# Block sums in the order in which they are read, each step with its own place, and the fourth and fifth groups' attention at new places, with whole exponentials

## The chip, the core and the metric

One core of one Trainium2 chip runs the whole kernel. The time is the device time of one execution in microseconds (us); three runs of the kernel before were taken, and one more was profiled. Engines: PE is TensorE (PEld its weight loads), DVE is VectorE, ACT is ScalarE, POOL is GpSimd, and SP issues the transfers. Each engine works through its own list of instructions in order.

## What is computed

```python
# 8 x 8 heads of 576 x 64, cut in chunks of 64 rows
scores = scale * np.matmul(q_c, k_c.transpose(0, 1, 2, 4, 3))
scores = scores - np.max(scores, axis=-1, keepdims=True)
attn = np.exp(scores)
attn = attn / (np.sum(attn, axis=-1, keepdims=True) + 1e-09)
out = np.matmul(attn, v_c)
# its result, 4608 tokens x 512, goes through
h = x @ w_in                # 512 -> 2048
g = h - np.tanh(h)
return g @ w_out            # 2048 -> 512
```

## The kernel before

**Groups, units and slots.** The 4608 tokens are nine groups of 512; `g` counts them from 0, so that the fourth group has `g` = 3 and the fifth `g` = 4. Each group's attention is worked out beside the feed-forward products of the group before it, and the feed-forward products fill PE. From group 2 on they go in *units*: a unit is half a group (256 tokens, `b` = 0 or 1) times a pair of 128-wide pieces of the inner dimension (`j` = 0 to 7), 16 units to a group. Unit `s` is the `s`-th of them, counted from 0 at group 2: group 3's units are 16 to 31, group 4's begin with 32. A unit has a first product (`gemm1`, L701, or `seven`, L716), then on ACT the tanh (L735), on DVE `g = h - tanh(h)` (L742, `shrink`), on POOL three instructions that add and subtract quarters of it (L743 to L745), on ACT and DVE the two float16 halves of the result (L754 and L755, `split`), and some units later the second product (`gemm2`, L774). The first product has two buffers `ph`: the product of unit `s + 2` waits for L742 of unit `s`. The second product goes through blocks that need seven products in place of eight.

**The block sums.** From unit 34 on, the first product goes by seven in place of eight too. It needs sums of blocks of the first weights, eight of them (`j` = 0 to 7), which `Half.seven` makes in seven steps each: two additions on POOL (L549, L551), two more POOL instructions (L554, L555), two more with a cast on ACT (L557, L558, L570), a difference on DVE with a store to memory (L566, L568), another cast (L574), and another difference and store. Seven of the eight are read back later, two units ahead of their use (`load`, L864); the eighth stays. Working room are two `temporary` pairs of pieces and three `stream` pairs, which from unit 34 on take in the sums that are read back.

**The order.** It is written by hand. `at` is a table of slots: slot `32 + 2 s` is worked off behind the first product of unit `s`, slot `33 + 2 s` behind its second product. `ahead` puts the attention steps of groups 2 and 3 at slots, `beside` those of groups 4 to 8. Within an engine nothing overtakes: a cast that stands ahead of a tanh holds the tanh up until what it waits for is there. SP's list holds the transfers in the same order.

**Attention of one half group** has the steps `scores` (PE, L351), `largest` (DVE, L363), `shifted` (DVE, L375), `exponent` (ACT, L379), `totals` (DVE, L385 to L389), `divided` (DVE, L393), `high` (ACT, L399), `transpose` (DVE L404, and two transposing transfers on SP, L408, into `aT`), `split_high` and `split_low` (halves of v), `values` (PE, L351, three products) and `blocks`, `differences`, `rounded` (the result as blocks, on ACT and POOL). For group 4 alone `shifted` and `exponent` are replaced by `by_row`: 16 instructions on ACT, one for each 64 columns, each of which takes its bias from the maximum and gives its sum too (L371, two rows of the trace each).

The line that decides who gets which room:

```python
made_in[j] = half.seven(j, temporary[1 - i % 2] if i else stream[2], stream[i % 2] if j < FC // 2 - 1 else temporary[1], j == FC // 2 - 1)
```

and the steps' places, 6.5 slots apart from sum to sum: `(13 * i - 43) // 2 + k for k in (0, 1, 2, 4, 5, 6, 7)`, where `i` = `j`.

Of the kernel before, what the change touches and what calls it, by code (L numbers as in the profile page):

```python
# [11 lines left out]
F32 = mybir.dt.float32  # L12
# [7 lines left out]
AX = mybir.AxisListType  # L20
# [39 lines left out]
def attn_ffn_kernel(ctx: ExitStack, tc: tile.TileContext, qE, kE, vE, qL, kL, vL, w_in, w_out, out):  # L60
# [211 lines left out]
    class Late:  # L272
# [86 lines left out]
        def largest(self, g, b):  # L359
            d = self.st[g, b]  # L360
            mx = d["mx"] = self.pool.tile([P, 16, 1], F32, name="mx", bufs=2)
            d["s"] = d["ps"].rearrange("p c e hp k -> p (c e hp) k")
            nc.vector.reduce_max(out=mx[:, :, 0], in_=d["s"], axis=AX.X)  # L363
            if g == SEVEN:
                nc.vector.tensor_scalar_mul(mx, mx, -scale)
                d["sm"] = self.pool.tile([P, 16, 1], F32, name="sm", bufs=2)

        def by_row(self, g, b, some):
            d = self.st[g, b]
            for n in some:  # L370
                nc.scalar.activation(d["s"][:, n], d["s"][:, n], AF.Exp, bias=d["mx"][:, n], scale=scale, accum_out=d["sm"][:, n])  # L371

# [53 lines left out]
        def blocks(self, g, b):  # L426
# [248 lines left out]
    class Fast:  # L675
# [251 lines left out]
        def ending(self):  # L927
# [39 lines left out]
            store(nc.scalar, 0, left)  # L967

    def in_seven(g, b, j):
        return (g, b, j // 2) != (SEVEN, 0, 0) and (g, b, j // 6) != (NG - 1, 1, 1)  # L970

    def beside(att, at, g):

        o = 2 * FC * (g - FAST)

        def put(unit, part, f, *args):
            at[o + 2 * unit + part].append(lambda: f(*args))

        put(-4, 0, att.halves, g, 0)
        late = g == SEVEN  # L980
        put(4 - 2 * late, late, att.halves, g, 1)
        put(10, 0, lambda: powers.update({g: half.power_of(g)}))
        for b, u in enumerate((3, 11)):
            first = g == SEVEN and not b
            put(u + 1 + first, 1, att.scores, g, b)
            put(u + 2 + first, 0, att.largest, g, b)
            if g == SEVEN:
                slots = range(2 * first + 1, 6)
                for i, k in enumerate(slots):
                    some = range(16 * i // len(slots), 16 * (i + 1) // len(slots))  # L990
                    put(u + 2 + k // 2, k % 2, att.by_row, g, b, some)
            else:
                put(u + 3, 0, att.shifted, g, b)
                put(u + 3, 1, att.exponent, g, b)
            put(u + 4 + (g == SEVEN), 0, att.totals, g, b)
            put(u + 5, 0, att.divided, g, b)
            put(u + 5, 1, att.high, g, b)
            put(u + 6, 0, att.transpose, g, b)
            put(u + 6, not first, att.split_high, g, b)
            put(u + 7 - first, first, att.split_low, g, b)  # L1000
            put(u + 8, 0, att.values, g, b)
            put(u + 8, 1, att.blocks, g, b)
            put(u + 9, 0, att.differences, g, b, 0)
            put(u + 9, 1, att.differences, g, b, 1)
            put(u + 10, 1, att.rounded_high, g, b, 1)
            put(u + 10, 1, att.rounded_low, g, b, 1)
            put(u + 11, 1, att.rounded_high, g, b, 0)
            put(u + 11, 1, att.rounded_low, g, b, 0)
            if g + 1 < NG:
                for i in range(2):  # L1010
                    p = FIRST[g + 1] + 2 * b + i, 2 * b + i
                    put(u + 2 + i, 1, att.load, *p, "q")
                    put(u + 4 + i, 1, att.load, *p, "k")
                    put(u + 7, 1, att.load, *p, "v")
        put(6 - late, late, att.spread, g)
        put(6 - late, 1, att.greatest, g)

    def ahead(att, at, g):
# [9 lines left out]
        late, before = g == FAST, g == SEVEN - 1
        if not late:
            put(-3, 0, att.halves, g, 0)  # L1030
            put(3, 1, att.halves, g, 1)
        put(4 if late else 6, -0.5 if late else 0, att.spread, g)
        put(4 if late else 6, -0.5 if late else 1, att.greatest, g)
        put(14 if late else 9, 1, lambda: powers.update({g: half.power_of(g)}))
        put(6, 0, lambda: xs.update({g: new_half_x()}))
        for b, u in enumerate((3, 13) if late else (6, 14)):
            spaced = late and not b
            other = u + 3 if spaced else u + 2 if late else u + 1
# [3 lines left out]
            u += late - before * (1 + b)  # L1042
            put(u + 2, before and b, att.scores, g, b)
            for i in (2 * b, 2 * b + 1):
# [6 lines left out]
            else:  # L1051
# [306 lines left out]
```

## Time and profile before

| | us |
|---|---|
| median of three runs | 790.15 (788.72 to 790.75) |
| the profiled execution, its time | 790.28 |
| the profiled execution, its span | 788.0 |
| PE busy | 769.9 |
| POOL busy | 531.7 |
| DVE busy | 627.8 |
| ACT busy | 497.8 |

The span runs from the first instruction to the last; 2.3 us of the execution lie around it. In rows of the trace a line such as L742 is a line of the kernel before; `x24` counts merged instructions; what stands in brackets is idle time ahead of the instruction and what ended it. PEclk 1.00 is TensorE's clock at 2.4 GHz, and a stretch of 0.93 had some of its time at 1.2 GHz. A matmul's duration is from its start to its modelled end, so two that follow each other overlap in the rows; the time that one costs is the distance of two starts.

### The profile page before, as it was taken

Reading aid. Unit: us, or ns where it says so; the run is one execution under the profiler, and the core shown is the slowest. Engines: PE = TensorE matmul, PEld = TensorE weight load, DVE = VectorE, ACT = ScalarE, POOL = GpSimd, SP = SyncE. Lnnn points to the kernel's source line nnn. Section 1 sums busy time; section 2 is a strip of 40 time slices with the busy share of each in tenths; the row PEclk is TensorE's granted clock in tenths of the full one; section 3 lists DMA queues with packets and bytes.
Section 4 is the critical chain, followed back from the end, with each engine's and each line's share of the span. In section 5 each row is a group of like instructions: output and inputs, shape, how many; then the busy total and the mean of one; then the engine's idle time right before and its main releaser. Section 6 shows DMA issues by size and latency. Waiting matters only on the chain.

```text
span 788.0 us, 23812 instructions
## 1 busy us (share of the span) xinstructions
PE 769.9 (98%) x10037; PEld 666.5 (85%) x10037; DVE 627.8 (80%) x1034; ACT 497.8 (63%) x862; POOL 531.7 (67%) x598
## 2 busy tenths in 40 slices
PE   8999999999999999979899999999999999999997
PEld 4878885666788888868799999999999999999996
DVE  5896998888698898667578797979797979796665
ACT  6887988556465454573856666666666666666553
POOL 1100002586678888869786979797979796979763
PEclk9999999999999999999999999999999999999999
DMA  9854441210232233234254545455545452435120
GB/s 349 320 188 161 161 161 53 82 27 2 81 81 96 81 115 89 67 66 136 82 166 148 161 135 163 134 162 128 167 130 155 151 176 65 154 61 155 55 83 28
DMA packets 78059, 98.02 MB, mean 124 GB/s; under 512 B 34944, under 2 KB 42112, under 8 KB 77952
## 3 DMA queue, kind: packets, MB, share of 16 engines
q1 hardware_dynamic: 77520, 95.84, 39.3%
q8 instruction: 79, 1.29, 0.7%
q10 hardware_dynamic: 432, 0.66, 0.2%
q14 instruction: 28, 0.23, 0.1%
HBM read 76.02 MB, written 13.11 MB: 113 GB/s over the span
## 4 chain that ended last, share of the span: by engine, by line
PE 48%; POOL 4%; DVE 2%; issue 1%; ACT 1%; DMA 0%; POOLq 0%; DVEq 0%; ACTq 0%
PE ph L716 23%; PE po L774 22%; PE psa L351 2%; PE po L938 1%; POOL xl L743 1%; PE ph L701 1%; POOL wl L443 1%; POOL xh L452 0%; DMA aT<-a 0%; POOL xl L745 0%; POOL wh L558 0%; POOL xh L437 0%; ACT wl L754 0%; DVE xl L742 0%; POOL xl L744 0%
## 5 line engine op out<-in xcount | busy, mean ns | idle before, releaser
L743 POOL TENSOR_TENSOR xl<-xl 128x256 f32<-128x256 f32 x111 | 153.3, 1381 | 93.5 <-DVE xl L742 93.2
L735 ACT ACTIVATE t<-ph,sig 128x512 f32<-128x512 f32 x112 | 77.0, 687 | 138.5 <-DVE ph L731 113.9
L716 PE MATMUL ph<-xh,wl 128*128 128x128 f16 x1608 | 115.3, 220 | 2.5 <-DVE xl L742 2.5
L716 PE MATMUL ph<-xh,wh 128*128 128x128 f16 x1530 | 110.9, 220 | 0.3 <-DVE ph L726 0.3
L742 DVE SCALAR_TENSOR_TENSOR xl<-ph,sig,t 128x512 f32<-128x512 f32 x112 | 83.2, 742 | 25.3 <-ACT t L735 25.1
L716 PEld LDWEIGHTS <-wl 128*128 128x128 f16 x1608 | 96.4, 98 | 3.3 <-issue 2.7
L716 PEld LDWEIGHTS <-wh 128*128 128x128 f16 x1530 | 95.2, 98 | 3.1 <-DVE ph L726 1.4
L774 PEld LDWEIGHTS <-gh 128*128 128x128 f16 x924 | 88.0, 98 | 11.1 <-issue 1.5
L701 PE MATMUL ph<-xh,wh 128*128 128x256 f16 x804 | 94.4, 275 | 0.9 <-DVE xl L742 0.9
L774 PEld LDWEIGHTS <-wl 128*128 128x128 f16 x882 | 85.5, 98 | 9.7
L755 DVE SCALAR_TENSOR_TENSOR gl<-xl,to_g,gh 128x896 f16<-128x896 f32 x68 | 83.5, 1228 | 8.4 <-ACT gh L754 8.4
L774 PE MATMUL po<-wl,gh 128*128 128x256 f16 x610 | 88.1, 273 | 0.9 <-DVE wl L787 0.9
L701 PEld LDWEIGHTS <-wh 128*128 128x128 f16 x804 | 78.8, 99 | 11.3 <-issue 1.6
L745 POOL TENSOR_TENSOR xl<-xl 128x256 f32<-128x256 f32 x111 | 83.4, 752 | 0.0
L754 ACT ACTIVATE gh<-xl,to_g 128x896 f16<-128x896 f32 x68 | 70.9, 1043 | 19.7 <-POOL xl L745 19.4
L774 PE MATMUL po<-wl,wl 128*128 128x256 f16 x549 | 82.1, 273 | 0.0
L725 DVE TENSOR_TENSOR ph<-ph,t 128x128 f32<-128x128 f32 x76 | 22.7, 299 | 59.0 <-ACT t L721 58.6
L774 PE MATMUL po<-wh,wl 128*128 128x256 f16 x333 | 60.0, 274 | 0.0
L755 DVE SCALAR_TENSOR_TENSOR wl<-xl,to_g,wl 128x896 f16<-128x896 f32 x44 | 54.7, 1244 | 6.3 <-ACT wl L754 6.3
L615 PE MATMUL ph<-xh,wh 128*128 128x512 f16 (+2 forms) x252 | 59.3, 377 | 0.4 <-ACT xh L269 0.4
L744 POOL TENSOR_TENSOR xl<-xl 128x128 f32<-128x128 f32 x111 | 59.2, 533 | 0.0
L754 ACT ACTIVATE wl<-xl,to_g 128x896 f16<-128x896 f32 x44 | 45.9, 1042 | 19.1 <-POOL xl L745 18.0
(235 smaller groups left out, 1680.2 us busy)
## 6 DMA issues: line engine op xcount, KB each, us to landing
wl<-kept SPq DMA_DIRECT2D x118, 256.0 KB, 3.6
raw<-w_in SPq DMA_DIRECT2D x16, 512.0 KB, 3.7
raw<-w_out SPq DMA_DIRECT2D x16, 512.0 KB, 5.1
xl<-qL SPq DMA_DIRECT2D x28, 256.0 KB, 3.8
rawv<-vL SPq DMA_DIRECT2D x28, 256.0 KB, 2.9
rawk<-kL SPq DMA_DIRECT2D x28, 256.0 KB, 4.6
out<-wl SPq DMA_DIRECT2D x55, 128.0 KB, 1.9
kept<-wl SPq DMA_DIRECT2D x14, 256.0 KB, 2.3
```

What stands on the lines that cost most here:

```text
L615: nc.tensor.matmul(ph, lhsT=w[:, kc * P:(kc + 1) * P], rhs=x[b][:, kc, cols], start=(k == 0), stop=(k == 3 * KC - 1))
L701: nc.tensor.matmul(self.ph[:, 1 - f::2, :], lhsT=half_w[fc][:, w, kc * P:(kc + 1) * P], rhs=rhs, start=(k == 0), stop=(k == 3 * KC - 1))
L716: nc.tensor.matmul(ph[:, o], lhsT=a[:, w, i * P:(i + 1) * P], rhs=x[v][:, m, i * P:(i + 1) * P], start=(n == "P5" and k == i == 0), stop=( ...
L725: nc.vector.tensor_add(ph[:, 3], ph[:, 3], c[:, 2])
L735: nc.scalar.activation(t, self.ph, AF.Tanh, scale=self.powers[0])
L742: nc.vector.scalar_tensor_tensor(out=u[:, :4], in0=self.ph, scalar=sig, in1=t, op0=ALU.mult, op1=ALU.subtract)
L743: engine.tensor_add(u[:, 4:6], u[:, 1:3], u[:, 0:4:3])
L744: engine.tensor_add(u[:, 6], u[:, 1], u[:, 2])
L745: engine.tensor_sub(u[:, 0:4:3], u[:, 0:2], u[:, 2:4])
L754: nc.scalar.activation(gh, u, AF.Copy, scale=powers[1])
L755: nc.vector.scalar_tensor_tensor(out=gl, in0=u, scalar=powers[1], in1=gh, op0=ALU.mult, op1=ALU.subtract)
L774: nc.tensor.matmul(place[m], lhsT=part[:, self.SUM[m]], rhs=w[m][:, o], start=first, stop=(last and part is gl), skip_group_check=True)
```

## The change

The sums are made in the order 2, 3, 4, 5, 6, 7, 0, 1, in which the fifth group's first half reads them, each step at a slot of its own and with its own two rooms (`SUMS`; counted from slot 64). The attention steps of groups 3 and 4 get tables of slots (`FOURTH`, counted from slot 32, and `FIFTH`, from 64). Groups 5 to 8 (`LATER`) and group 2 keep their slots. `by_row` goes: group 4 has `shifted`, one `exponent` and `totals` with its own sum like the others. The room of group 4's first result is `stream[1]` in place of `stream[2]`.

```diff
             nc.vector.reduce_max(out=mx[:, :, 0], in_=d["s"], axis=AX.X)
-            if g == SEVEN:
-                nc.vector.tensor_scalar_mul(mx, mx, -scale)
-                d["sm"] = self.pool.tile([P, 16, 1], F32, name="sm", bufs=2)
-
-        def by_row(self, g, b, some):
-            d = self.st[g, b]
-            for n in some:
-                nc.scalar.activation(d["s"][:, n], d["s"][:, n], AF.Exp, bias=d["mx"][:, n], scale=scale, accum_out=d["sm"][:, n])
...
-            if g != SEVEN:
-                d["sm"] = self.pool.tile([P, 16, 1], F32, name="sm", bufs=2)
-                nc.vector.reduce_sum(out=d["sm"][:, :, 0], in_=d["s"], axis=AX.X)
-            sm = d["sm"]
+            sm = d["sm"] = self.pool.tile([P, 16, 1], F32, name="sm", bufs=2)
+            nc.vector.reduce_sum(out=sm[:, :, 0], in_=d["s"], axis=AX.X)
...
-            d["f"] = [place_of(*n, F32) for n in (stream[2] if (g, b) == (SEVEN, 0) else temporary[0])]
+            d["f"] = [place_of(*n, F32) for n in (stream[ROOM] if (g, b) == (SEVEN, 0) else temporary[0])]
...
+    FOURTH = {'halves': [-6, 7], 'spread': [12], 'greatest': [13], 'power': [17], 'room': [10], 'split': [19, 31], 'scores': [14, 29], 'load_qk': [14, 32], 'largest': [15, 29], 'shifted': [15, 29], 'exponent': [18, 30], 'totals': [18, 32], 'divided': [20, 32], 'high': [22, 34], 'transpose': [23, 35], 'values': [27, 41]}
+    SUMS = {2: (2, 0, [-21, -21, -19, -17, -10, -9, -7]), 3: (3, 1, [-14, -14, -13, -12, -8, -8, -7]),
...
+    ROOM = 1
...
-    def make_in(i, j):
+    def make_in(j):
         if j not in made_in:
-            made_in[j] = half.seven(j, temporary[1 - i % 2] if i else stream[2], stream[i % 2] if j < FC // 2 - 1 else temporary[1], j == FC // 2 - 1)
+            temp, place = SUMS[j][:2]
+            made_in[j] = half.seven(j, *((stream + temporary)[i] for i in (temp, place)), j == FC // 2 - 1)
         next(made_in[j])
...
-    steps = [[(13 * i - 43) // 2 + k for k in (0, 1, 2, 4, 5, 6, 7)] for i in range(FC // 2)]
...
+    for j, (_, _, steps) in SUMS.items():
+        for k in steps:
+            at[o + k].append(lambda j=j: make_in(j))
```

Three places on the engines, as the two programs order them. Behind line 380 the lines of the kernel after stand 10 lower: its tanh is L725, its splits L744 and L745, its `shrink` L732, the casts of a sum L560 and L564, `high` L389.

ACT from unit 23's tanh (L735) to unit 25's, before. `psa` are the scores, a cast L570 or L574 belongs to a sum, L399 is `high`, L330 and L331 come behind unit 25's split:

```order
L735 ACTIVATE t<-ph,sig 128x512
L754 ACTIVATE wl_2496<-xl,to_g 128x896
L371 ACTIVATE psa,sm<-psa,mx 128x64 x11
L570 CAST wl_4521<-wh_4383 128x512
L735 ACTIVATE t<-ph,sig 128x512
L754 ACTIVATE wl_2498<-xl,to_g 128x896
L399 CAST a<-psa 128x2x8x64
L574 CAST wl_4520<-wh_4382 128x512
L735 ACTIVATE t<-ph,sig 128x512
L754 ACTIVATE gh<-xl,to_g 128x896
L330 ACTIVATE rawv<-rawv,to 128x1024
L331 CAST wl_1707<-rawv 128x1024
```

and now, from the whole exponential (L371) at the end of unit 22 on; the first cast is that of sum 7, the second of sum 0:

```order
L371 ACTIVATE psa<-psa 128x1024
L725 ACTIVATE t<-ph,sig 128x512
L744 ACTIVATE wl_2496<-xl,to_g 128x896
L564 CAST wh_4426<-wl_4134 128x512
L725 ACTIVATE t<-ph,sig 128x512
L744 ACTIVATE wl_2498<-xl,to_g 128x896
L560 CAST wl_4559<-wh_4454 128x512
L330 ACTIVATE rawv<-rawv,to 128x1024
L331 CAST wl_1707<-rawv 128x1024
L725 ACTIVATE t<-ph,sig 128x512
L744 ACTIVATE gh<-xl,to_g 128x896
L389 CAST a<-psa 128x2x8x64
```

The 11 rows of the exponential between unit 23's split and unit 24's tanh are gone; `split_high` (L330, L331) stands ahead of unit 25's tanh, `high` (L389) behind it.

DVE in units 31 and 32, before: L566 is a sum's difference, L387 to L389 finish the totals, L393 divides, L404 makes the low half that is transposed, the second L742 is unit 32's:

```order
L742 SCALAR_TENSOR_TENSOR xl<-ph,sig,t 128x512
L755 SCALAR_TENSOR_TENSOR wl_2497<-xl,to_g,wl_2496 128x896
L566 TENSOR_TENSOR wh_5113<-wh_4924,wh_5113 128x512
L387 TENSOR_SCALAR sm<-sm 128x16
L388 RECIPROCAL sm<-sm 128x16
L389 TENSOR_SCALAR sm<-sm 128x16
L393 TENSOR_TENSOR psa<-psa,sm 128x1024
L755 SCALAR_TENSOR_TENSOR wl_2499<-xl,to_g,wl_2498 128x896
L404 TENSOR_TENSOR a<-psa,a 128x2x8x64
L742 SCALAR_TENSOR_TENSOR xl<-ph,sig,t 128x512
```

and now:

```order
L732 SCALAR_TENSOR_TENSOR xl<-ph,sig,t 128x512
L745 SCALAR_TENSOR_TENSOR wl_2497<-xl,to_g,wl_2496 128x896
L376 TENSOR_REDUCE sm<-psa 128x16
L377 TENSOR_SCALAR sm<-sm 128x16
L378 RECIPROCAL sm<-sm 128x16
L379 TENSOR_SCALAR sm<-sm 128x16
L383 TENSOR_TENSOR psa<-psa,sm 128x1024
L745 SCALAR_TENSOR_TENSOR wl_2499<-xl,to_g,wl_2498 128x896
L732 SCALAR_TENSOR_TENSOR xl<-ph,sig,t 128x512
L394 TENSOR_TENSOR a<-psa,a 128x2x8x64
```

The sum's difference is gone from here, the totals have their own sum over the row (L376), and unit 32's `shrink` (now L732) stands ahead of the low half (now L394).

ACT in unit 18, where the second half of group 2 is finished (L789 to L794), before:

```order
L735 ACTIVATE t<-ph,sig 128x512
L754 ACTIVATE gh<-xl,to_g 128x896
L574 CAST wl_3957<-wh_3825 128x512
L789 ACTIVATE wl_3249<-po_3484,undo_g 128x512
L790 ACTIVATE wh_3250<-po_3485,undo_g 128x256
L794 ACTIVATE wl_2493<-po_3486,undo_g 128x256
L735 ACTIVATE t<-ph,sig 128x512
```

and now:

```order
L744 ACTIVATE gh<-xl,to_g 128x896
L779 ACTIVATE wl_3246<-po_3480,undo_g 128x512
L780 ACTIVATE wh_3247<-po_3481,undo_g 128x256
L784 ACTIVATE wl_2493<-po_3482,undo_g 128x256
L564 CAST wl_3829<-wl_3692 128x512
L560 CAST wl_4066<-wh_3901 128x512
L725 ACTIVATE t<-ph,sig 128x512
```

The cast of a sum (L574) stood ahead of the three readings of `po`, and now two such casts stand behind them.

## Rows read from the trace of the kernel before

**Rows 1.** PE's waits by releaser, 228 to 400 us (total, times, longest)

```profile
PE psa L351 <- DVE wl L340: 2.6, 1, 2.6
PE ph L716 <- DVE xl L742: 2.5, 1, 2.5
PE psa L351 <- issue: 1.4, 1, 1.4
PE psa L351 <- DMA aT<-a: 1.1, 2, 0.9
PE po L774 <- DVE wl L787: 0.9, 2, 0.7
PE ph L701 <- DVE xl L742: 0.9, 1, 0.9
```

**Rows 2.** Windows: busy us of PE, PEld, DVE, ACT, POOL, PEclk, DMA share, GB/s

```profile
375.00:400.00 25.00, 22.46 (x229) 20.25 (x230) 15.76 (x23) 18.33 (x48) 20.02 (x24) 0.93 0.36 101
400.00:750.00 350.00, 350.00 (x5864) 329.70 (x5864) 281.71 (x512) 220.12 (x326) 288.64 (x320) 1.00 0.46 136
```

**Rows 3.** PE's timeline, 290 to 405 us: start, us, instruction, [idle before]

```profile
321.79 2.78 PE L701 MATMUL ph<-xh,wh 128*128 128x256 f16 x24
...
326.70 2.78 PE L701 MATMUL ph<-xh,wh 128*128 128x256 f16 x24
...
354.76 0.64 PE L351 MATMUL psa<-aT,wl 64*64 64x64 f16 x32 [0.86 <-DMA aT<-a]
355.34 4.10 PE L701 MATMUL ph<-xh,wh 128*128 128x256 f16 x24
...
392.32 0.80 PE L716 MATMUL ph<-xh,wl 128*128 128x128 f16 x6 [2.54 <-DVE xl L742]
...
397.50 0.50 PE L716 MATMUL ph<-xh,wh 128*128 128x128 f16 x6
397.84 1.17 PE L716 MATMUL ph<-xh,wl 128*128 128x128 f16 x18
```

**Rows 4.** ACT's timeline, 335 to 405 us

```profile
338.81 0.69 ACT L735 ACTIVATE t<-ph,sig 128x512 f32<-128x512 f32 x1
```

**Rows 5.** DVE's timeline, 335 to 405 us

```profile
349.00 1.21 DVE L404 TENSOR_TENSOR a<-psa,a 128x1024 f16<-128x1024 f32 x1
```

**Rows 6.** ACT's groups by form, 240 to 400 us: busy, mean ns | idle before

```profile
L754 ACT ACTIVATE wl<-xl,to_g 128x896 f16<-128x896 f32 x15 | 15.6, 1041 | 15.1 <-POOL xl L745 15.1
...
L371 ACT ACTIVATE psa<-psa,mx 128x64 f32<-128x64 f32 x32 | 9.2, 286 | 4.6 <-DVE mx L365 3.8
...
L574 ACT CAST wl<-wh 128x512 f16<-128x512 f32 x6 | 3.7, 619 | 8.7 <-POOL wh L558 8.7
...
L330 ACT ACTIVATE rawv<-rawv,to 128x1024 f32<-128x1024 f32 x2 | 2.3, 1143 | 0.0
...
L379 ACT ACTIVATE psa<-psa 128x1024 f32<-128x1024 f32 x2 | 2.0, 1010 | 0.4 <-DVE psa L375 0.4
```

**Rows 7.** DVE's groups by form, 240 to 400 us

```profile
L742 DVE SCALAR_TENSOR_TENSOR xl<-ph,sig,t 128x512 f32<-128x512 f32 x27 | 20.1, 744 | 19.8 <-ACT t L735 19.7
...
L755 DVE SCALAR_TENSOR_TENSOR gl<-xl,to_g,gh 128x896 f16<-128x896 f32 x12 | 15.1, 1258 | 3.0 <-ACT gh L754 3.0
L566 DVE TENSOR_TENSOR wl<-wh,wl 128x512 f16<-128x512 f32 x12 | 14.6, 1214 | 0.0
...
L375 DVE TENSOR_TENSOR psa<-psa,mx 128x1024 f32<-128x1024 f32 x2 | 2.5, 1232 | 0.1
```

**Rows 8.** POOL on tile xl, 240 to 400 us: min/median/max ns, first and last start

```profile
L743 POOL TENSOR_TENSOR xl<-xl x28: 714/1170/1582, 240.6 to 396.9; 128x256 f32<-128x256 f32 x28
L744 POOL TENSOR_TENSOR xl<-xl x28: 443/453/1313, 241.3 to 398.5; 128x128 f32<-128x128 f32 x28
L745 POOL TENSOR_TENSOR xl<-xl x28: 719/723/1711, 241.7 to 398.9; 128x256 f32<-128x256 f32 x28
```

**Rows 9.** POOL's groups by form, 240 to 400 us

```profile
L549 POOL TENSOR_TENSOR wh<-wh 128x512 f32<-128x512 f16 x7 | 8.1, 1150 | 0.0
```

More of the change, by code (lines that the diff above doesn't have):

```diff
@@ L972, in beside @@
     def beside(att, at, g):
[L974 to L1008, printed above, removed]
@@ new lines, in beside, with put @@
+        o, keys = 2 * FC * (g - FAST), FIFTH if g == SEVEN else LATER
+        def put(name, f, *args, half=0, nth=0):
+            k = keys[name][half]
+            k = k[nth] if isinstance(k, tuple) else k
+            at[o + k].append(lambda: f(*args))
+        for b in range(2):
+            put("halves", att.halves, g, b, half=b)
+        put("power", lambda: powers.update({g: half.power_of(g)}))
+        for b in range(2):
+            for name in ("scores", "largest", "shifted", "exponent", "totals", "divided", "high", "transpose", "split_high", "split_low", "values", "blocks"):
+                put(name, getattr(att, name), g, b, half=b)
+            for i in range(2):
+                put("differences", att.differences, g, b, i, half=b, nth=i)
+            for i in range(2):
+                for part in "high", "low":
+                    put("rounded", getattr(att, "rounded_" + part), g, b, 1 - i, half=b, nth=i)
@@ L1011, in beside @@
                     p = FIRST[g + 1] + 2 * b + i, 2 * b + i
[L1012 to L1016, printed above, removed]
+                    for n in "qkv":
+                        put("load_" + n, att.load, *p, n, half=b, nth=i)
+        put("spread", att.spread, g)
+        put("greatest", att.greatest, g)
     def ahead(att, at, g):
@@ L1026, in put, with place @@
             at[o + 2 * unit + part].append(lambda: f(*args))
[L1028 to L1034, printed above, removed]
+        if g == SEVEN - 1:
+            def place(name, f, *args, half=0):
+                at[o + FOURTH[name][half]].append(lambda: f(*args))
+            for b in range(2):
+                place("halves", att.halves, g, b, half=b)
+            place("spread", att.spread, g)
+            place("greatest", att.greatest, g)
+            place("power", lambda: powers.update({g: half.power_of(g)}))
+            place("room", lambda: xs.update({g: new_half_x()}))
+            for b in range(2):
+                place("split", att.split, g, b, half=b)
+                for i in (2 * b, 2 * b + 1):
+                    place("split", att.load, FIRST[g + 1] + i, i, "v", half=b)
+                place("scores", att.scores, g, b, half=b)
+                for i in (2 * b, 2 * b + 1):
+                    place("load_qk", att.load, FIRST[g + 1] + i, i, "qk", half=b)
+                for name in ("largest", "shifted", "exponent", "totals", "divided", "high", "transpose"):
+                    place(name, getattr(att, name), g, b, half=b)
+                at[o + FOURTH["values"][b]].insert(0, lambda b=b: (att.values(g, b), att.result(g, b)))
+            return
+        put(4, -0.5, att.spread, g)
+        put(4, -0.5, att.greatest, g)
+        put(14, 1, lambda: powers.update({g: half.power_of(g)}))
         put(6, 0, lambda: xs.update({g: new_half_x()}))
-        for b, u in enumerate((3, 13) if late else (6, 14)):
-            spaced = late and not b
-            other = u + 3 if spaced else u + 2 if late else u + 1
+        for b, u in enumerate((3, 13)):
+            spaced = not b
+            other = u + 3 if spaced else u + 2
             put(other, -0.5 if spaced else 1, att.split, g, b)
@@ L1041, in ahead @@
                 put(other, 1, att.load, FIRST[g + 1] + i, i, "v")
-            u += late - before * (1 + b)
-            put(u + 2, before and b, att.scores, g, b)
+            u += 1
+            put(u + 2, 0, att.scores, g, b)
             for i in (2 * b, 2 * b + 1):
```

13 lines of the change are left out of this document (6 added, 7 removed).

## The prediction

> **What bounds the kernel now.** I read the windows first, then PE's waits, then the timelines around them. From 400 to 750 us PE is busy 350.00 of 350 us at full clock, with DVE busy 282 and POOL 289 [rows 2]: nothing can be won there unless products are left out, and the change leaves none out. What can be won lies before 400 us, where PE waits eight times, 9.4 us in all [rows 1], and where its clock fell twice.
>
> The waits say who was late. In the first half of group 4, unit 24's tanh begins at 338.81 [rows 4]. That unit's first product started 4.91 after unit 23's at 326.70 and took 2.62 (24 products, 0.109 apart: 4.91 is 45 of them), so it was done at 334.2: the tanh was 4.6 late, with 11 rows of the exponential ahead of it on ACT. Behind it everything on ACT and DVE slid: a `ph` was still in use (0.9, L742), then the low half of v was missing (2.6, L340), then the transposed low half of the scores (0.9 of the 1.1, aT) [rows 1, 3]. In the second half the same 16 rows end as 2.5 us before unit 34's product (L742), and 1.4 + 0.9 fall around 307 to 320 us, in unit 18's finish and behind it.
>
> The clock: the 24 products at 355.34 take 4.10 where the same took 2.78 at 321.79 [rows 3], 1.3 more, right behind the long wait; and from 392.32 to 397.50 there are 24 small products (0.0557 apart: 6 take 0.34 from 397.50 to 397.84) and 21 of 0.109, 3.6 at full clock, which took 5.2: 1.6 more, right behind the 2.5 us wait. The window there shows 0.93 [rows 2]: some of it at 1.2 GHz.
>
> A third piece hides in how rows are drawn: a matmul's end is modelled 0.16 behind the next one's possible start (24 × 0.109 = 2.62 against 2.78), so each of eight waits costs 0.16 more than its bracket, 1.3. **All that can go: 9.4 + 2.9 + 1.3 = 13.6 us.** The profiled execution took 790.28, 0.13 above the median, so the floor is 776.7 there and 776.6 by the median.
>
> **What the change does to these, part by part.**
>
> *The exponential in one.* 32 rows L371 of 0.286 and as many readings of the sum go from ACT; two L379 of 1.01 come [rows 6]. DVE gets, twice, one L375 of 1.23 [rows 7] and one row sum of the same 1024 columns, taken alike, less one small multiplication: about 2 us each time. DVE hides it as long as L742 is in time: it sat idle 19.8 us ahead of 27 of them [rows 7], and a `shrink` may end 7.2 - 1.4 = 5.8 us after its product's end plus tanh and itself before the product after the next one wants its `ph` (2.29 + 2.62 + 2.29 between them).
>
> *First half of group 4, counted from unit 22's first product (0).* Without waits unit 27's first product ends at 5 × 4.91 + 2.62 = 27.2, and the three `values` products follow at once: that is the deadline. Durations are the groups' means, tanh 0.69 and split 1.04 on ACT, L742 0.74 and L755 1.26 on DVE [rows 4, 6, 7], about 0.1 less where instructions follow closely. DVE: unit 22's L742 ends at 4.1, the split of 21 at 5.5, maximum and shift at 7.9, two differences of sums at 10.1, L742 of 23 at 10.8. ACT: exponential to 9.0, tanh 23 to 9.6 (due 7.5, allowed to be 5.8 late). DVE goes on: split 11.9, totals 14.2, a difference 15.3, L742 of 24 at 16.0, split 17.1, division 18.3. POOL: 23's three instructions and the next sum's three end at 16.1, whereupon ACT casts it (16.6), splits v (18.7), does tanh 25 (19.3), split 20.3 and `high` 21.3; DVE's low half of the scores ends at 22.6 and that of v at 24.3. In the trace the last wait for aT ended at 354.76, 4.6 after L404 ended at 350.2 [rows 3, 5]; so aT is whole at 27.2, just at the deadline. The `ph` wait and the v wait are gone with 3 to 4 us to spare; the wait for aT is 0 give or take 1.5. I take 0.5 of it as left. It must not bring the clock down: behind the 0.9 us wait before unit 27's product [rows 1] no stretch ran slow.
>
> *Unit 18.* ACT's cast L574 sat 8.7 us idle in six of them for POOL's L558 [rows 6]; one stood ahead of the readings of `po`. Two casts now stand behind them and need sums that POOL finished a unit before. The readings come about 2 us earlier, and with them L742, POOL and group 3's last result: 0.9 and 1.4 go. The price, two casts of 0.62 ahead of tanh 19, lies within the 5.8.
>
> *Second half of group 4.* Unit 34's product is due 12 × 4.91 + 2.0 (scores and `values`) = 60.9 after 0. Its `ph` needs L742 of unit 32, which now stands ahead of the low half, with no rows and no difference before it. POOL sets it: the four `differences` and the two `rounded_low` (about 3.5 and 4) push unit 31's three instructions to 55.6; split on ACT, tanh 32, L742: 58.6. 2.3 to spare, so 2.5 us and the slow clock behind it go.
>
> *Sums and POOL.* The same 48 instructions, but seven units (20 to 26) now carry 18 of them: 18 × about 1.0 (L549 takes 1.15, the smaller ones less [rows 9]), 7 × 2.35 for the three of L743 to L745 at their medians [rows 8], and 2.4 for a finish make 37 against 34.4. POOL falls 3 us behind; its result is asked for a unit later (the split, then a second product three units on), so PE does not see it.
>
> *Group 3.* PE lost 0.2 there. The transposes move from slot 52 to 55 with `values` still at 59: 9.8 us for 4.6 and what DVE is late. 0.
>
> *SP.* Loads of q and k move ahead of those of v, and the read-back of the third sum now waits for POOL's rounding (room `stream[1]`) ahead of the second half's transposes. By the reckoning above POOL rounds at 53, `high` is ready at 58: nothing waits. If POOL were 5 us later, the transposes would slip the same 5 minus 2.7 of slack at `values`.
>
> **Sum.** 790.28 - 13.6 + 0.5 = 777.2, by the median 777.0.
>
> **Rivals.**
>
> *The gap at the first `values` stays.* For it: aT meets its deadline with nothing to spare on a chain of some 25 instructions, and DVE has 12 us of work in the 12 us from 4 to 16. Then 2 to 3.7 us of waiting come back, and the slow clock behind them, 1.3: 3.3 to 5.0 on the floor of 776.7, **780.0 to 781.7**; with the `ph` wait too (0.9 and its 0.2), 782.8.
>
> *It moves and does not go.* For it: every step stands in another row, and lateness before went from ACT to DVE to PE. Both large gaps stay with their clock, and only unit 18's 2.3 + 0.3 go: **787.7**, within 0.3% (2.4 us), which is about what a measurement of this kernel can tell from no change. Against it: the cause, ACT's rows, is not there any more.
>
> *Slower: POOL sets the pace.* Its three instructions take 2.35 at the medians, but 4.6 at their longest [rows 8]. Sums, blocks and roundings now stand shoulder to shoulder from unit 20 to 31. Were all twelve units at the longest, POOL would lose 12 × 2.25 = 27; some 8 of it are hidden by the lag, and 19 against 13.1 gained make **796**. It decides from a mean of about 4.1 a unit on. Against it: half of the L744 and L745 are at 0.45 and 0.72. The rows show L743 between 0.71 and 1.58. The Trainium skill ("SBUF — State Buffer", section "SBUF: two separate sides") has a reason: DVE with two inputs in SBUF and POOL reading SBUF lock each other out for a whole instruction. By that rule the added shift and row sum, which read PSUM, would cost POOL nothing, while the 0 to 3 differences L566 more in these units would block it for up to 3 × 1.2, which alone gives 777 to 778. No row here has the two alone.
>
> **Chances.** Forecast 0.66 (775.0 to 779.5: below, the floor of 776.6 less the 1.4 by which the lowest of three runs lay under the median, rounded down; above, a wait of some 2.5 us without the slow clock); the gap stays 0.18; moves 0.08; POOL sets the pace 0.05; 0.03 for others, half of them faster than the floor by something not seen. The range 775.0 to 784.0 takes in the forecast and the first rival (782.8, and 1.2 for the spread of runs upward), 0.84. Faster by over 0.3%: 0.66 + 0.18 + 0.03 = 0.87; the same 0.08; slower 0.05.
>
> **What would show it.** Right: PE without a wait over 0.5 us from 260 to 750 us, no window under clock 1.00 there, unit 34's product starting near 378 in place of 392, tanh 24 within 1 us of its product's end, the last read of `po` in unit 18 followed by casts. Wrong: a wait of `values` for aT or v over 1.5 us (first rival), L742 or `ph` waits in units 27 to 34 (second), or POOL busy without a pause from 315 to 385 us with a mean of the three instructions over 4 us (third).

## The result, and the profile after

| | median of runs, us | lowest to highest | runs |
|---|---|---|---|
| before | 790.45 | 788.72 to 791.30 | 4 |
| changed | 778.45 | 778.03 to 779.02 | 4 |

The ratio is 0.985, with a 95% interval of 0.983 to 0.987: 12.0 us faster, where 13.1 was forecast (777.0, range 775 to 784). The profiled execution took 779.02 with a span of 776.1, 11.9 shorter than the span before. The same shows on PE alone, without what lies at the two ends of the span: from unit 0's first product to the last matmul of the program it took 555.2 us before (227.92 to 783.09) and 543.1 after (227.74 to 770.87), 12.0 less.

In the changed kernel every line after 379 stands 10 lower: the tanh is L725, shrink's DVE line L732, its POOL lines L733 to L735, the split L744 and L745, the products L691 and L706. Of PE's waits before 400 us, eight with 9.4 us [rows 1], and one of 0.3 near the end, these are left (220 to 760 us; total, times, longest):

```profile
PE psa L351 <- DMA aT<-a: 1.2, 2, 0.7
PE po L764 <- DVE wl L777: 0.3, 1, 0.3
PE ph L706 <- DVE ph L716: 0.3, 1, 0.3
```

The last one is that of 0.3, as before. The windows that answer to [rows 2], with PE busy, then PEld, DVE, ACT and POOL, and the granted clock:

```profile
375.00:400.00 25.00, 25.00 (x445) 23.18 (x443) 19.82 (x33) 15.14 (x23) 20.03 (x23) 1.00 0.57 166
400.00:750.00 350.00, 349.68 (x5727) 329.20 (x5725) 283.75 (x516) 219.28 (x323) 285.98 (x318) 1.00 0.46 135
```

No window up to 750 us is under 1.00 any more. PE's timeline of the changed kernel, at the places that answer to [rows 3] (start, us, instruction, [idle before]):

```profile
275.86 0.71 PE L351 MATMUL psa<-aT,wl 64*64 64x64 f16 x64 [0.71 <-DMA aT<-a]
277.09 0.45 PE L351 MATMUL psa<-aT,wl 64*64 64x64 f16 x32 [0.52 <-DMA aT<-a]
...
320.48 2.79 PE L691 MATMUL ph<-xh,wh 128*128 128x256 f16 x24
...
345.06 2.78 PE L691 MATMUL ph<-xh,wh 128*128 128x256 f16 x24
347.77 0.98 PE L351 MATMUL psa<-aT,wl 64*64 64x64 f16 x96
...
381.65 0.50 PE L706 MATMUL ph<-xh,wl 128*128 128x128 f16 x6
```

All 96 products of group 4's first `values` now run in one piece, 27.3 behind unit 22's first product, and unit 34's product begins 61.2 behind it. What is new is at 275.86: group 3's first `values` wait for aT, 0.71 and 0.52. That is the place which the prediction priced at nothing.

### The profile page after: what moved, and what is told of

It reads as the page before. It is cut to its first block, busy times and chain, and to the rows that moved or that the text cites. A ratio compares the mean times of both kernels' runs of the same rounds, so it can differ in the third digit from the quotient of the medians.

```text
span 776.1 us, 23750 instructions
## 1 busy us (share of the span) xinstructions
PE 764.6 (99%) x10034; PEld 663.8 (86%) x10037; DVE 633.1 (82%) x1036; ACT 486.9 (63%) x800; POOL 532.5 (69%) x598
## 4 chain that ended last, share of the span: by engine, by line
PE 89%; DVE 5%; DMA 2%; ACT 2%; POOL 1%; issue 1%; SPq 0%; POOLq 0%; ACTq 0%; DVEq 0%
PE po L764 30%; PE ph L706 23%; PE ph L691 11%; PE po L636 10%; PE ph L605 9%; PE psa L351 4%; PE psa L186 1%; PE po L928 1%; DMA raw<-w_out 1%; DMA q<-qE 1%; DMA aT<-a 0%; DVE wl L745 0%; PE psa L247 0%; DVE w L144 0%; ACT s L221 0%
## 5 line engine op out<-in xcount | busy, mean ns | idle before, releaser
L733 POOL TENSOR_TENSOR xl<-xl 128x256 f32<-128x256 f32 x111 | 150.4, 1355 | 80.1 <-DVE xl L732 79.9
L725 ACT ACTIVATE t<-ph,sig 128x512 f32<-128x512 f32 x112 | 77.0, 687 | 145.6 <-DVE ph L721 114.8
L706 PE MATMUL ph<-xh,wl 128*128 128x128 f16 x1608 | 114.7, 219 | 0.0
L706 PE MATMUL ph<-xh,wh 128*128 128x128 f16 x1530 | 110.3, 219 | 0.3 <-DVE ph L716 0.3
L706 PEld LDWEIGHTS <-wh 128*128 128x128 f16 x1530 | 94.6, 98 | 3.1 <-DVE ph L716 1.4
L764 PEld LDWEIGHTS <-gh 128*128 128x128 f16 x924 | 88.0, 98 | 10.2 <-issue 0.5
L706 PEld LDWEIGHTS <-wl 128*128 128x128 f16 x1608 | 95.9, 98 | 0.6
L691 PE MATMUL ph<-xh,wh 128*128 128x256 f16 x804 | 93.1, 273 | 0.0
L745 DVE SCALAR_TENSOR_TENSOR gl<-xl,to_g,gh 128x896 f16<-128x896 f32 x68 | 84.3, 1239 | 9.9 <-ACT gh L744 9.9
L732 DVE SCALAR_TENSOR_TENSOR xl<-ph,sig,t 128x512 f32<-128x512 f32 x112 | 83.1, 742 | 10.0 <-ACT t L725 9.8
L691 PEld LDWEIGHTS <-wh 128*128 128x128 f16 x804 | 78.1, 98 | 9.7 <-issue 0.5
L744 ACT ACTIVATE gh<-xl,to_g 128x896 f16<-128x896 f32 x68 | 70.9, 1042 | 24.1 <-POOL xl L735 22.5
L735 POOL TENSOR_TENSOR xl<-xl 128x256 f32<-128x256 f32 x111 | 81.7, 736 | 0.0
L745 DVE SCALAR_TENSOR_TENSOR wl<-xl,to_g,wl 128x896 f16<-128x896 f32 x44 | 57.6, 1309 | 6.8 <-ACT wl L744 6.8
L744 ACT ACTIVATE wl<-xl,to_g 128x896 f16<-128x896 f32 x44 | 45.9, 1042 | 20.7 <-POOL xl L735 17.0
```

What stands on the lines that cost most here:

```text
L691: nc.tensor.matmul(self.ph[:, 1 - f::2, :], lhsT=half_w[fc][:, w, kc * P:(kc + 1) * P], rhs=rhs, start=(k == 0), stop=(k == 3 * KC - 1))
L706: nc.tensor.matmul(ph[:, o], lhsT=a[:, w, i * P:(i + 1) * P], rhs=x[v][:, m, i * P:(i + 1) * P], start=(n == "P5" and k == i == 0), stop=( ...
L725: nc.scalar.activation(t, self.ph, AF.Tanh, scale=self.powers[0])
L732: nc.vector.scalar_tensor_tensor(out=u[:, :4], in0=self.ph, scalar=sig, in1=t, op0=ALU.mult, op1=ALU.subtract)
L733: engine.tensor_add(u[:, 4:6], u[:, 1:3], u[:, 0:4:3])
L735: engine.tensor_sub(u[:, 0:4:3], u[:, 0:2], u[:, 2:4])
```

## The experiments

The change has three parts that can be had apart: the exponentials in one (E), the sums' order, steps and places with their room (S), and the new slots of groups 3 and 4 (T; in the code FOURTH and FIFTH). Order, steps and places of the sums were not taken apart from each other. All eight combinations exist; medians, and in brackets what E is worth at that place:

| | slots before | slots new |
|---|---|---|
| sums before, by row | 790.25 (kernel before) | 787.50 |
| sums before, E | 788.52 (-1.7) | 782.89 (-4.6) |
| sums new, by row | 784.50 | 782.57 |
| sums new, E | 780.11 (-4.4) | 778.45 (-4.1) |

Alone the three give 1.7, 5.8 and 2.8, 10.2 in sum; all at once give 12. E is worth 1.7 alone, and 4.1 to 4.6 wherever one of the others stands beside it. The kernel before stood at 790.25, 789.32, 790.57 and 788.95 in the four sets of runs that follow, so that 1 us between sets means nothing.

A part of these medians is PE's clock and not the order. Each execution has its mean granted clock on record: 0.992 to 0.998 in every one of the kernel before for which it is listed, 0.999 or 1.000 in those of the change, and both in three of the combinations. The sums alone took 782.67 at 1.000 and 784.30 to 785.54 below it, the slots alone 785.33 at 1.000 and 787.29 to 788.51 below it, the change with the old sums 782.17 and 782.23 at 1.000, 783.54 and 784.71 below it. At full clock throughout, E is worth 2.6 beside the new sums (782.67 to 780.11) and 3.1 beside the new slots (785.33 to 782.20), the first number of each pair from one execution, and 4.1 beside both. So E is worth more beside the others than alone, but by less than the table says, and the sum of 10.2 depends on how often the clock fell.

The `diff` blocks of this section give each edit in short, not the lines of the programs.

**Without the exponentials in one.** Where `by_row` is put back, `totals` loses its row sum again for this group.

```diff
-  "shifted", "exponent"                 (group 4)
+  by_row: 16 rows in three pieces at slots 13, 14, 14; in five at 28 to 31
```

> The changed kernel, with the fourth group of the fast part (the program's SEVEN) again taking its exponentials by row: 16 rows of 0.29 us on ACT for each half, at the slots of the one exponential (first half) and at slots 28 to 31 (second); DVE loses the shift and the row sum. Theory A (ACT's rows are what made PE wait): the first half has 4.6 us on ACT where 1.0 stands, 3.6 late against a deadline met with nothing to spare, less the 2.4 us that DVE no longer does ahead of totals: 1 to 3.5 us of waits at the first values or the ph behind them come back, with 1.3 of half clock where one is over 2.5, so 780 to 784. Theory B (the places in the tables are what counts): PE sees nothing, 778 to 779.

Measured 782.57 (782.31 to 782.88; ratio to before 0.991, 0.989 to 0.994), 4.1 more than the change. PE's timeline of this run, where `by_row` moves the numbers back (L774 the second product, L716 the small ones):

```profile
352.39 0.60 PE L774 MATMUL po<-wl,gh 128*128 128x256 f16 x4 [0.31 <-DVE wl L787]
353.69 0.81 PE L774 MATMUL po<-wl,gh 128*128 128x256 f16 x6 [0.70 <-DVE wl L787]
...
385.67 0.50 PE L716 MATMUL ph<-xh,wl 128*128 128x128 f16 x6 [2.35 <-DVE xl L742]
```

3.4 of waits and three restarts of 0.16 are 3.8 of the 4.1. So the size is theory A's, the place is not: the first `values` of group 4 don't wait at all here, 1.0 falls close behind them (L787), and it is unit 34's `ph` that is late. New slots and new sums together cover these `values` even with 16 rows on ACT; either one without the other doesn't (1.6 and 1.3, and 1.4, in two runs below).

**Only the exponentials in one**, in the kernel before.

```diff
-  by_row at slots 13 to 15 and 27 to 31
+  shifted at 13 and 27, exponent at 14 and 28, and the row sum in totals
```

> The kernel before, with nothing changed but the exponentials of that group: one shift on DVE, one exponential on ACT and one row sum on DVE, at the slots where the first rows stood. Theory A: the waits of 2.6, 0.9, 0.9 and most of the 2.5 us go with their half clock, 6 to 9 us in all; unit 18's waits (0.7 and 1.4) stay: 781 to 784. Theory B: 788 to 790.

Measured 788.52 (788.15 to 790.27, 10 runs; ratio 0.9986, 0.9976 to 0.9997, or 1.1 us): theory B's number. The rows by themselves are not the cause on which I had laid the lateness. The waits (PE's, 228 to 400 us; numbers 5 lower than before):

```profile
PE ph L711 <- DVE xl L737: 2.9, 1, 2.9
PE psa L351 <- issue: 1.4, 1, 1.4
PE psa L351 <- DMA aT<-a: 1.2, 1, 1.2
PE psa L351 <- DVE wl L340: 1.2, 1, 1.2
PE po L769 <- DVE wl L782: 0.9, 2, 0.7
PE psa L351 <- DVE xh L419: 0.3, 1, 0.3
```

Unit 34's wait has even grown, from 2.5 to 2.9, and the first `values` still wait 2.4. What took the rows' place there, ACT's timeline shows:

```profile
334.92 1.03 ACT L749 ACTIVATE wl<-xl,to_g 128x896 f16<-128x896 f32 x1
341.49 1.01 ACT L394 CAST a<-psa 128x1024 f16<-128x1024 f32 x1 [5.54 <-DVE psa L388]
342.40 0.62 ACT L569 CAST wl<-wh 128x512 f16<-128x512 f32 x1
342.92 0.69 ACT L730 ACTIVATE t<-ph,sig 128x512 f32<-128x512 f32 x1
```

and DVE's, of the same run:

```profile
335.06 0.75 DVE L737 SCALAR_TENSOR_TENSOR xl<-ph,sig,t 128x512 f32<-128x512 f32 x1 [2.66 <-ACT t L730]
335.99 1.57 DVE L750 SCALAR_TENSOR_TENSOR wl<-xl,to_g,wl 128x896 f16<-128x896 f32 x1 [0.18 <-ACT wl L749]
337.48 1.21 DVE L381 TENSOR_REDUCE sm<-psa 128x16 f32<-128x1024 f32 x1
...
340.23 1.23 DVE L388 TENSOR_TENSOR psa<-psa,sm 128x1024 f32<-128x1024 f32 x1
```

The rows are gone, and ACT stands idle for 5.54 us: the cast of the scores' high half is next in its order and waits for DVE's row sum and division, which stand behind a shrink and a split of DVE's. Unit 25's tanh, two places behind the cast, begins 3.9 after its product's end (336.37 + 2.62 = 338.99). In the kernel before, the rows made unit 24's tanh 4.6 late; here the old slots make the next one late by nearly as much. This second link could be read before the change: there ACT stood idle ahead of the same cast, until DVE's division ended at 344.33 (L393, 343.10 and 1.23).

```profile
344.41 1.01 ACT L399 CAST a<-psa 128x1024 f16<-128x1024 f32 x1 [3.98 <-issue]
```

**The change with the old sums.**

```diff
-  SUMS 2..7, 0, 1 with steps of their own; ROOM = 1
+  0..7, steps (13 i - 43) // 2 + (0, 1, 2, 4, 5, 6, 7), old places; ROOM = 2
```

> The changed kernel, with the block sums in the old order (0 to 7), at the old steps 6.5 slots apart and in the old places. Theory A (the sums' places are what freed unit 18): the waits of unit 18's finish and of the scores behind it, 2.3 with restarts, come back, and nothing else: 780.5 to 781. Rival: the sums' old steps also push POOL and ACT in the fourth group, whose values or ph waits come back: 782 to 786. Second rival: the sums are worth nothing, 778 to 779.

Measured 782.89 (782.17 to 784.71; 0.992, 0.989 to 0.994). Unit 18's two waits are back as theory A has it, 0.7 and 1.1, and with them a third, a `ph` wait in the fourth group as the rival has it, with the rival's number:

```profile
PE ph L706 <- DVE xl L732: 3.2, 1, 3.2
PE psa L351 <- DVE xh L414: 1.1, 1, 1.1
PE po L764 <- DVE wl L777: 0.7, 1, 0.7
```

The 3.2 is unit 34's `ph` again, with the exponentials in one and the new slots in place. DVE's timeline ahead of it:

```profile
375.78 1.38 DVE L745 SCALAR_TENSOR_TENSOR wl<-xl,to_g,wl 128x896 f16<-128x896 f32 x1
379.23 0.98 DVE L556 TENSOR_TENSOR wh<-wh,wh 128x512 f16<-128x512 f32 x1 [2.07 <-ACT wh L564]
380.15 1.22 DVE L376 TENSOR_REDUCE sm<-psa 128x16 f32<-128x1024 f32 x1
...
384.65 0.74 DVE L732 SCALAR_TENSOR_TENSOR xl<-ph,sig,t 128x512 f32<-128x512 f32 x1
```

and POOL's:

```profile
374.61 1.61 POOL L442 TENSOR_TENSOR xh<-wl,xh 128x512 f16<-128x512 f32 x1
376.17 1.57 POOL L547 TENSOR_TENSOR wh<-wh,wh 128x256 f32<-128x256 f32 x1
377.82 0.73 POOL L548 TENSOR_TENSOR wh<-wh 128x256 f32<-128x256 f32 x1
```

The last sum's difference L556 stands ahead of the row sum in DVE's order; it waits 2.07 for ACT's cast, which waits for POOL's L548, which stands behind a rounding. In the kernel before the same difference (there L566) stood between the same neighbours. So a sum that is finished late is enough to hold unit 34 up, rows or not: it waits in all four kernels with the old sums (2.5 before, 2.9, 3.2, and 3.5 with the slots alone). With the new sums rows are enough in the new slots (2.35 in the first run), not in the old ones (0.3 in the next). In the changed kernel the sums are over before this place.

**Only the sums**, in the kernel before.

```diff
-  make_in(i, j) for the eight in order
+  the change's SUMS, make_in(j) and the room stream[1]
```

> The kernel before, with nothing changed but the sums: new order, steps and places, and the room of the first blocks. Theory A: unit 18's two waits go, 2.3: 787.5 to 788.5. Rival: the nearer sums crowd the fourth group, which is still late by its rows: 790 to 793.

Measured 784.50 (782.67 to 785.54; 0.993, 0.991 to 0.996), a larger gain than either expectation. Unit 18's 2.1 became 1.4 (0.67 and 0.75). What I had not laid on the sums is unit 34: its wait fell from 2.5 to 0.3. Of the first half's waits L340's 1.6 and aT's 1.3 are left. A new one for the scores, 1.1, stands at 281.56, where the kernel before waits for nothing.

**The slots alone, and the two other parts without them.**

```diff
 slots only:  by_row as in the first run, sums as in the third
 two parts:   FOURTH and FIFTH with the slots of the kernel before
```

> The changed kernel, with the exponentials by row and the old sums: the kernel before with the new slots and nothing else. If the new slots are worth what undoing them cost (1.5 less 0.4): 789 to 790. If they cure the first values by themselves (the run with rows kept had no wait for v or aT there): the 2.6, 0.9 and 0.9 us of waits and one half clock go and unit 18's and unit 34's stay: 784 to 786.

> The changed kernel, with the slots of groups 3 and 4 of the fast part all as before: the kernel before with the exponentials in one and the new sums, and nothing else. If the two parts only add (1.8 and 5.8 alone): 782.7. If they need each other (either one alone leaves unit 34's ph late, so that only both together free it): 778.5 to 780.5, with waits for aT or v of 0.3 to 2 us left.

Slots only: 787.50 (785.33 to 788.51; 0.997, 0.996 to 0.998), with L340's wait 1.4 in place of 2.6, aT's gone, unit 34's up to 3.5 and a new 1.4 just ahead of it; neither of the two numbers. Two parts: 780.11 (779.94 to 780.73; 0.987, 0.986 to 0.989), the number expected of parts that need each other: unit 34 waits no more. The waits that are left are not those expected: none is for aT or v in group 4, where 0.7 is left for L777, and 1.1, 0.65 and 0.5 stand at 282, 306 and 320 us.

**The tables one by one.**

```diff
 old fourth:  FOURTH split 15, room 12, power 19, divided 18, high 20, transpose 20, ...
 old fifth:   FIFTH shifted 13, 27; exponent 14, 28; high 17, 33; split_low 19, 36; ...
```

> The changed kernel, with group 3's steps at their old slots. Theory A (the moved transposes of group 3 are the cause of the new wait of 1.2 us for aT at its first values): the wait goes and nothing comes: 776.5 to 777.3. Rival (the move bought something that the trace of the change cannot show, such as unit 18's finish or the scores behind it): that wait of 0.7 to 1.4 comes back, 778 to 780.

> The changed kernel, with the fifth group's steps at their old slots (exponentials still in one, the shift and the exponential at the slots of the first rows). Theory A (exponentials and sums did it, the new slots of the fifth group little): 778 to 779.5. Rival (its new slots are what keeps the second half's ph and the first values in time): waits of 2 us or more come back in units 25 to 34, with half clock behind one over 2.5: 781 to 785.

Old fourth: 778.01 (777.85 to 778.12), 0.4 less than the change: its wait for aT is gone, as theory A has it, and 0.9 for the scores at 281.80 and 0.45 at 319.44 came in its place, as the rival has it. Group 3's new slots buy nothing that shows. Old fifth: 780.01 (779.76 to 780.23), 1.6 more than the change, 2.0 more than old fourth in the same set, and the same as without both tables: it is FIFTH that is worth something. Its waits are not the 2 us and more in units 25 to 34 of the rival: 1.6 for aT at 276.91, in group 3, and 0.3 at group 4's first `values`, with 0.6 for L777 close behind.

**Mending the new wait.** SP's timeline of the changed kernel, ahead of 275.86:

```profile
269.52 2.44 SPq L794 DMA_DIRECT2D out<-wl  x4
272.06 0.41 SPq L558 DMA_DIRECT2D kept<-wl  x1
272.55 2.67 SPq L398 DMA_TRANSPOSE aT<-a  x2
```

The first transpose needs only the high half, which ACT had ready at 267.26, the second the low half, ready at 271.18 (DVE's L394, begun at 269.97, 1.21):

```profile
266.24 1.02 ACT L389 CAST a<-psa 128x1024 f16<-128x1024 f32 x1
```

Both stand behind the four stores of group 2's end, which waited for POOL until 269.5, and the write of a sum's half (L558; the expectation calls it a read-back). They left at 272.6 and 273.9 and landed 3.1 to 3.3 us later, when PE began. By an estimate from these rows a free queue would have had both landed by 274.5, ahead of the 275.15 at which the products were due. I moved the transposes ahead, with the steps that feed them, and then one sum step; as division and cast move too, these runs do not part the queue from DVE:

```diff
-  FOURTH  'divided': [20, 32], 'high': [22, 34], 'transpose': [23, 35]
+  FOURTH  'divided': [18, 32], 'high': [20, 34], 'transpose': [20, 35]
   and in the second run also
-  SUMS    3: (3, 1, [-14, -14, -13, -12, -8, -8, -7])
+  SUMS    3: (3, 1, [-14, -14, -13, -11, -8, -8, -7])
```

> The changed kernel, with three steps of group 3's first half moved: the division at slot 18 in place of 20, the high half at 20 in place of 22, the transposes at 20 in place of 23, so that they stand ahead of the four stores of group 2's end and of a sum's read-back on SP, and ahead of the sum's cast on ACT. Theory A (the wait for aT of 0.7 and 0.5 is queueing behind these): aT comes 5 us or more earlier, the two waits and their restarts go, 1.5: 776.9. Rival (DVE bounds it, and the division only takes the place of work that PE needs): an L732 or L777 is 1.2 later and PE waits there in its place, 778 to 779.

> As the run with three moved steps, and one step of the sum of unit 3 moved as well, from slot -12 to -11, so that its cast on ACT, which waits 3.6 us for POOL, stands behind the readings of po that PE's next product waits for. Theory A: the 0.35 us wait for L777 and its restart go too, 776.4. Rival: the cast is late for the sum's low half, and POOL's queue shifts the wait to another unit: 776.9 or more.

Measured 777.83 (777.51 to 777.95) and 777.70 (777.58 to 777.91). With the first edit both old waits are gone, aT's and L777's, so that the second had nothing left to win; in both runs the next scores wait, in the second by this row:

```profile
282.19 1.16 PE L351 MATMUL psa<-rawk,xl 64*64 64x64 f32 x64 [1.53 <-DVE xh L414]
```

1.6 removed (0.71, 0.52 and 0.35), 1.4 to 1.5 handed on. The scores want the bank that L414 reads, and ACT's and DVE's parts of that reading stood behind two sum steps. Those were moved next, and in a last run two more ahead of unit 18:

```diff
-  SUMS 3: ... -8, -8, -7]      4: ... -7, -6, -4 ...
+  SUMS 3: ... -8, -8, -5]      4: ... -7, -5, -4 ...
   and in the last run also
-  SUMS 5: ... -2, 3, 5, 5]     6: [0, 0, 3, 5, ...
+  SUMS 5: ... -2, 5, 5, 5]     6: [0, 0, 3, 7, ...
```

> As the run with three moved steps and one moved sum step, and two sum steps of group 3's slots moved behind the reading of the first values: the cast of sum 4 from slot -6 to -5 (it held ACT for POOL 1.2 us ahead of L412) and the second low half of sum 3 from -7 to -5 (1.2 us of DVE ahead of L414). Theory: the 1.5 us wait of the next scores for DVE's L414, which took the place of the waits for aT, shrinks to 0.1 to 0.4, and no PE wait is left from 228 to 740 us: 776.2 to 776.6. Rival (that gap moves once more, to the shift or a ph behind the moved low half): 777.2 to 777.8.

> As the run with two more sum steps moved behind the reading of the first values, and two more: the first low half of sum 5 from slot 3 to 5 (1.2 us of DVE ahead of the L732 that unit 19's product waits for, 0.41) and the second step of POOL's finishing of sum 6 from 5 to 7 (2.2 us of POOL ahead of unit 18's three instructions, whose split stands ahead of the L414 that the scores wait for, 0.50). Theory (each wait is one queue's order, and a step behind the instruction asked for costs nothing): both waits go with their restarts, 1.2: 776.2 to 776.4, with no PE wait from 228 to 740 us. Rival (DVE, with 1.2 more behind unit 18's finish, hands the wait on): 777.2 to 778.

The first gave 777.41 (777.33 to 777.63; ratio to before 0.984, 0.982 to 0.985), the fastest of all: every run of it lies under every run of the change, by 1.0 in the median, which is less than the 0.3% that a comparison of two kernels from different sets can vouch for. The wait at 282 is gone; 0.4 and 0.5 came at 304.71 and 318.81. The last gave 777.79 (777.50 to 777.87): those two shrank to 0.35 in all, and the first `values` of group 4 waited, the place where the prediction had its deadline with nothing to spare:

```profile
318.06 1.16 PE L351 MATMUL psa<-rawk,xl 64*64 64x64 f32 x64 [0.35 <-DVE xh L414]
348.09 0.45 PE L351 MATMUL psa<-aT,wl 64*64 64x64 f16 x32 [0.89 <-DMA aT<-a]
```

Its rival has the number right, not the way. DVE stood no later than in the run before when it came to unit 25's `shrink` (its last difference ahead of it begins at 338.69, there at 338.92), but here it idled 1.75 for the tanh: ACT's cast of a sum, three places ahead of that tanh, waited longer for POOL. The cast in the run before and in this one, and DVE's `shrink` in this one:

```profile
336.76 0.62 ACT L560 CAST wl<-wh 128x512 f16<-128x512 f32 x1 [2.08 <-POOL wh L545]
```

```profile
338.04 0.62 ACT L560 CAST wl<-wh 128x512 f16<-128x512 f32 x1 [3.00 <-POOL wh L545]
341.41 0.75 DVE L732 SCALAR_TENSOR_TENSOR xl<-ph,sig,t 128x512 f32<-128x512 f32 x1 [1.75 <-ACT t L725]
```

## Why the prediction held, point by point

- **All that can go, 13.6.** Slightly small. In the fastest run PE takes 542.4 from unit 0's first product to the last matmul (227.87 to 770.30), with 0.91 of waits and two restarts of 0.16 in it that the floor would not have: 541.2, which is 14.0 under the kernel before.
- **Unit 18, 2.3 and restarts.** Right, but for 0.2 of the 2.3, which stood at 266 us in group 3: no wait is left at 307 to 320 us, and with the old sums 0.7 and 1.1 come back.
- **First half of group 4.** Right in the outcome, in part by luck: tanh 24 starts at 333.20, 0.3 behind its product's end (4.91 ahead of 335.23, and 2.62); the low half of the scores was to end 22.6 after unit 22's first product and that of v at 24.3, and they end at 23.7 and 25.3 (DVE's L394 at 342.94 + 1.21, L340 at 344.07 + 1.73, less 320.48), each 1 us late. With the 4.6 that I took for aT from there it would have missed its deadline by 1. It met it, and the 0.5 was not lost, because the second transpose landed 3.1 after its issue, where it had taken 4.5 in the kernel before.
- **Second half, unit 34.** Right that 2.5 and the slow clock go. The margin was too rosy: L732 of unit 32 was to end 2.3 ahead of the product, it ended at 381.0 (380.25 and 0.75), 0.65 ahead of 381.65. The sign "near 378" for that product doesn't follow from the sum: 392.32 less the 9.4, 1.3 and 1.3 that stand ahead of it is 380.3, and 381.65 was measured. With 16 rows or the old sums in addition that is overdrawn, as both runs show.
- **Group 3: "0".** This is the term of the sum that failed, and with it the sign "without a wait over 0.5 us from 260 to 750 us". I counted 9.8 us from transposes to `values` for 4.6 of work "and what DVE is late", and looked at DVE alone; the queue that carries the transposes was taken by stores and a write until 272.55, 5.3 after the high half was ready and 1.4 after the low half. It cost 1.23 of waits and two restarts, and L777's 0.35 ahead of it stayed with its restart: 2.1 of the 14.0, which leaves 11.9 where 12.0 was measured.
- **What the rows alone are worth.** The sum never asked for it, but the text laid the lateness on ACT's rows ("the cause, ACT's rows, is not there any more"). Taken alone they are worth 1.7 of 12; the division's place holds ACT behind them, and the late sums hold unit 34. The change removes three things that each hid the others.
- **POOL sets the pace** (the slower rival). Not so: from 315 to 385 us POOL is busy 63.2 of 70, with L733 to L735 at 2.5 in the mean, where the rival needed 4.1; L733's median is 0.73 from 240 to 400 us. No wait of PE's ends at POOL, but POOL reaches PE through ACT's casts: the 0.35 for L777 goes back to a cast that stood 3.60 for POOL ahead of the readings of `po` (L560 at 262.92), as did the 0.89 of the last run. What the Trainium skill ("SBUF — State Buffer", section "SBUF: two separate sides") says of the lock does show in the rows (below), mostly as a cost inside POOL's slack; whether it had a share in the 0.35 (the L545 ahead of that cast took 1.64, beside a split of DVE's) was not tried.

## What to carry to other kernels

Where an engine's order is written by hand, the waits' releasers name the last link of a chain, and two or three chains can end within a microsecond of each other: take each part alone and undo each part alone before saying what did it. A step that is moved must be walked through the queue that carries it, the DMA queue's own order included, not only through the engine that computes it. Near the floor a removed wait is handed to the next deadline: of four edits the first and the third removed the waits they aimed at, the second found its wait already gone, and the three won 1.0 us together; the fourth lost 0.4 of it, and steps of that size lie within the spread between sets.

## What the runs showed of the hardware

**The clock after a wait is not the same in every execution.** Ahead of unit 34 the runs had waits between 2.35 and 3.47 us, with PE at full clock before. In the kernel before, in the one with E alone and in the change with the old sums (2.54, 2.87, 3.17) the granted clock fell to 0.50 (1.2 GHz) behind it for some 3 to 6 us; in the run with rows kept (2.35) it stayed, and in the run with the slots alone it stayed behind 3.47. The windows behind the wait, first of the change with the old sums, then of the slots alone (PE busy, PEld, DVE, ACT, POOL, clock):

```profile
386.00:388.00 2.00, 2.00 (x22) 2.00 (x20) 0.53 (x1) 1.44 (x2) 2.00 (x4) 0.50 0.82 152
388.00:390.00 2.00, 2.00 (x12) 1.41 (x11) 1.25 (x4) 1.79 (x3) 1.38 (x1) 0.50 0.98 198
```

```profile
388.00:390.00 2.00, 1.10 (x20) 1.10 (x20) 1.98 (x3) 1.97 (x3) 1.07 (x2) 1.00 0.29 56
390.00:392.00 2.00, 2.00 (x25) 1.82 (x23) 0.63 (x3) 2.00 (x4) 2.00 (x3) 1.00 0.84 157
```

The execution of the slots alone that was profiled took 785.33 at a mean clock of 1.000; its six others have 0.994 to 0.998 on record and took 2.0 to 3.2 more. The two slow stretches of the kernel before had cost 1.3 and 1.6. So in one and the same kernel a long wait makes the fall possible and not certain. Nor is a single wait of more than 2.5, which two expectations name, needed for it: with E alone two waits of 1.18 and 1.20, 1.7 apart, had the 24 products behind them take 4.37 in place of 2.78, and the window from 354 to 356 us was at 0.53. In the kernel before it fell every time, by more or less (0.992 to 0.998), and its times follow that only loosely: 0.996 stands beside 788.64 and beside 791.04.

**POOL and DVE stand in each other's way, and the one that begins second pays.** In the changed kernel, 240 to 380 us, L733 (both operands in SBUF) took 0.72 to 0.73 in all eleven cases in which DVE was idle or at lines without two inputs in SBUF, and 0.72 to 1.64, 1.56 in the median, in the fifteen in which a DVE line with two inputs in SBUF (the split, a sum's difference or L340) overlapped it. In five of the fifteen POOL had begun first: L733 took 0.72 to 0.73 there, and DVE's line 1.57 to 1.73, where the split's most frequent time is 1.14. In the other ten DVE had begun first, and L733 took 1.17 to 1.64. Two neighbouring rows of POOL, and DVE's beside the first:

```profile
374.82 1.57 POOL L733 TENSOR_TENSOR xl<-xl 128x256 f32<-128x256 f32 x1
...
381.07 0.73 POOL L733 TENSOR_TENSOR xl<-xl 128x256 f32<-128x256 f32 x1 [3.59 <-DVE xl L732]
```

```profile
374.44 1.36 DVE L745 SCALAR_TENSOR_TENSOR wl<-xl,to_g,wl 128x896 f16<-128x896 f32 x1
...
380.91 1.22 DVE L394 TENSOR_TENSOR a<-psa,a 128x1024 f16<-128x1024 f32 x1
```

That is the lock of which the Trainium skill speaks ("SBUF — State Buffer", section "SBUF: two separate sides"); the trace agrees, and gives its price here: 0.4 to 0.9 us for L733 when it came second, most often 0.84, and 0.4 to 0.5 for DVE's split when that did.
